# A Fourier mixing layer and a feed-forward layer in one kernel: start-up copies and loads moved, one array laid out anew, batch one's steps renumbered

## The chip, the cores and the metric

The kernel runs on one core of one Trainium2 chip. The metric is the time of one execution in device microseconds (us). Three runs of the kernel before gave 785.98, 788.34 and 785.7 us; their median is 785.98. The core's engines are TensorE (PE in the profile; its weight loads are listed apart as PEld), VectorE (DVE), ScalarE (ACT), GpSimd (POOL) and SyncE (SP). In this kernel GpSimd and SyncE only start transfers (DMAs).

## The reference

For each of 8 batches, x has 3008 rows (the sequence) of 256 channels. The reference computes, in float32,

```
X = rfft(x, axis=1);  Y = X * (filt_r + 1j * filt_i);  y = irfft(Y, n=3008, axis=1)
t = y.reshape(24064, 256)
h = t @ w_in                              # 256 -> 2048
g = max(h, 0) + alpha * min(h, 0)         # alpha: one number for each of the 2048
out = g @ w_out                           # 2048 -> 256
```

The kernel works in 16-bit floats with float32 accumulation and writes float32.

## The kernel before, in words

**The transform.** The length 3008 is split as 94 x 32. Forward stage one is a product over the 94 (table `wf1`, for the first batch `wfx`); it gives 96 rows (48 frequencies, real and imaginary) for each of 32 positions. Then the array is turned so that the 32 positions lie across partitions. Stage two multiplies 64-by-64 blocks (table `twf`, forward), multiplies by the filter on VectorE, and multiplies back (tables `twi` and, for batch zero, `twx`). The result `v` is turned again into `zt`, and a last product over 96 rows (`wi3`) gives `yT`, the transformed tokens with channels across partitions, two batches at a time.

**Two ways to turn.** Batches one to seven (class `Fft`) turn their arrays through memory outside the core: `save_a` writes `a_dram`, `turn_a` reads it back turned; `turn_c` writes `v_dram` and, after the last part, reads `zt`. Batch zero (class `First`) has nothing to hide such trips behind, and turns on TensorE by products with an identity matrix: `turn_at` for the forward side, `half_t` and `piece_t` (through `turn`, line 346) for the inverse one. In both the array to be turned is the stationary operand, so it goes through a weight load.

**Batch zero, in order.** Eight forward pieces (`piece_a`, evicted by ScalarE and VectorE in turn) are made as x arrives. Between them stand warm-up products (`warm`) that compute nothing used. Then come `turn_at`, which moves two or four frequencies' columns from PSUM into `at`; twelve products `piece_b(kp)` (line 299), each followed by one VectorE multiplication by the filter (line 304); twelve products back `piece_c(kp)` (line 324); and `keep_c`, the evictions of their results into `v`. Products of stage two read the table `twd`, which is `twf` with each 32 columns written twice; `twice` makes it in three copies of eight frequencies each. Then `half_t` and `half_d` make a first part of `yT`, and the blocks begin. `piece_t` and `pair_d` of batch zero's other three groups run among the blocks.

**The blocks.** The feed-forward layer runs in 48 blocks of 512 (some 384) tokens, each of 16 steps. A step is one `up` (two products with `w_in`, line 478) and one part of `down` of the block before (products with `w_out`, line 509). Every second step ScalarE evicts two `up` results (line 487) and VectorE makes two products with alpha (line 490); every fourth step VectorE adds four at once (line 492). A batch's transform lies over 96 steps.

**What sets the order.** Nothing is scheduled by a tool: each engine's queue has the order in which the program is written. For the blocks a dictionary `plan` holds, for each step number, the pieces of the transforms to run there; `plan_fft` fills it from lists of steps: forward pieces (`a_at`), the turn (`ta`), loads of the next batch's x (`x_at`), products `piece_b` (`b_at`), `piece_c` (`c_at`, with `turn_c` one step after every second one), and inverse pieces (`d_at`). A piece runs ahead of its step's `up`; forward pieces and `piece_c` run behind the step's `down`, which then comes first.

**Buffers that matter here.** PSUM has eight banks: `hps` two buffers of two banks, `op` two of one, and one buffer `psF` of two. `psF` takes `turn_at`, `piece_t`, `pair_d` and, for batches one on, `piece_b`; there it is held until both VectorE multiplications (lines 186 and 187) have read it. The float32 tile `fst` holds the filter of the first frequencies and lies in the buffer `asb` of the later batches; it is copied into `filt_s` by a DMA on GpSimd's queue (line 428) after the twelve products, and released by that copy. Four copies into `filts_s` (line 431) and two within `filt_s` (line 433) follow on the same queue. `p_x` has four buffers for x.

**Markers.** A tiny `memset` on VectorE into the target of a load makes that load wait for the place that the memset has in VectorE's queue; the load then writes over it.

**Queues at the start.** SyncE's queue has the identity, `wfx`, the first third of `twf`, the eight parts of `fst`, the rest of `twf`, `twi` and `twx`, and small constants. GpSimd's has x of batch zero (eight parts), the filter (24 parts in three groups: frequencies 1 to 3, 4 to 7 and 8 to 11 in the kernel's count), `w_in` (two parts), `w_out` (two parts), x of batch one (eight parts), and the copies named above.

Of the kernel before, what the change touches and what calls it, by code (L numbers as in the profile page):

```python
# [15 lines left out]
NK = 24  # L16
# [34 lines left out]
def kernel(  # L51
# [10 lines left out]
    nc = tc.nc  # L62
# [46 lines left out]
    def load_x(b, c):  # L109
        xs = p_x.tile([N1, 8 * D], FP16, name="xs")  # L110
        for r in (slice(0, 48), slice(48, N1)) :
            nc.gpsimd.dma_start(out=xs[r], in_=xrow(b, c)[r])  # L112
        return xs
# [149 lines left out]
    class First(Fft):  # L263
# [61 lines left out]
                                             u[r, par, i, 128 * f : 128 * f + 128], t[r, 2 * kp + par],  # L325
                                             start=(i == 0), stop=(i == 1))

        def twice(self, ka, kb, copy):
            o = self.twd[:, ka:kb].rearrange("p k (i c m) -> p (k i) c m", i=2, c=2)
            w = twf_s[:, ka:kb].rearrange("p k (i m) -> p (k i) m", i=2)  # L330
            copy(o, w.unsqueeze(2).to_broadcast([128, 2 * (kb - ka), 2, 32]))

        def keep_c(self, kp, evicts, n=2):
            vm = self.vm.rearrange("p (g q k e) -> p g q k e", q=4, k=NK, e=4)
            for e in range(2):
                k = 2 * kp + e
                evicts[e](vm[:, :, :, k : k + 2 * n - 1 : 2],
                          self.ops[e][:, 0:n].rearrange("p k (g q e) -> p g q k e", q=4, e=4))

        def turn(self, pt, i, n):  # L340
            m = self.vm.rearrange("p (g m e) -> p g m e", m=96, e=4)
            for u in range(n):
                for f in range(2):
                    o = 256 * (u % 2) + 128 * f
                    s = n * i + u
                    nc.tensor.matmul(pt[0:96, u // 2, o : o + 128], m[:, 8 * f + s // 4, :, s % 4], id16,  # L346
                                     start=True, stop=True)
# [20 lines left out]
    f0 = First()  # L368
# [1 line left out]
    load_filt(nc.gpsimd, filt_s, 1, 4)  # L370
    load_filt(nc.gpsimd, filt_s, 4, 8)
    load_filt(nc.gpsimd, filt_s, 8, 12)
    for kt in range(2):
        nc.gpsimd.dma_start(out=win_s[:, kt], in_=moe_w_in[kt * 128 : (kt + 1) * 128])
    for q in range(2):
        nc.gpsimd.dma_start(
            out=wout_s[:, 8 * q : 8 * q + 8],
            in_=moe_w_out[1024 * q : 1024 * q + 1024].rearrange("(j p) d -> p j d", p=128))
    for c in range(4):
        xc[(1, c)] = load_x(1, c)  # L380

    def warm(n, pw):
        for _ in range(n):
            nc.tensor.matmul(pw.rearrange("p (r c) -> p r c", r=4), id16,
                             id16.unsqueeze(1).to_broadcast([128, 4, 128]), start=True, stop=True)

    warm(9, bank("o"))
    for i in range(8):
        f0.piece_a(i, both[i % 2], i % 3 < 2)
        if i % 2 == 1:  # L390
            warm((4, 4, 8, 3)[i // 2], bank("o"))
        if i == 1:
            nc.vector.memset(f0.fst[:, 0, :, 0:1], 0.0)
            load_filt(nc.sync, f0.fst, 0, 1)
        if i == 5:
            f0.twice(0, 8, on_act)
            nc.vector.memset(twf_s[:, 8:24, 0:1], 0.0)
            tables(nc.sync, ("twf",), 8, 24)
            tables(nc.sync, ("twi", "twx"), 0, 8)
            tables(nc.sync, ("twi", "twx"), 8, 24)  # L400
            nc.sync.dma_start(out=wi3_s, in_=consts["wi3"].ap())
            nc.sync.dma_start(out=al16, in_=moe_alpha.rearrange("(j p) -> j p", p=128))
            nc.sync.dma_start(out=id32, in_=id32_d.ap())
            nc.sync.dma_start(out=wf1_s, in_=consts["wf1"].ap())
            nc.sync.dma_start(out=sgn_s, in_=sgn_d.ap())
    f0.twice(8, 16, on_act)
    f0.twice(16, 24, on_dve)
    f0.turn_at(0, 1, on_act)
    f0.turn_at(1, 1, on_dve, True)
    warm(2, bank("o"))  # L410
    f0.piece_b(0)
    f0.turn_at(2, 2, on_act)
    f0.piece_b(1)
    warm(2, bank("o"))
    f0.turn_at(4, 2, on_act)
    for kp in range(12):
        if kp < 10:
            f0.piece_b(kp + 2)
        f0.piece_c(kp)
        if kp > 9:  # L420
            f0.keep_c(kp, (on_act, on_act) if kp == 10 else both, 1)
        elif kp % 2 == 1:
            f0.keep_c(kp - 1, (on_act, on_act))
            if kp < 7:
                f0.turn_at(kp + 5, 2, on_act)
        if 7 <= kp < 10:
            warm(2, banks(False)[:, 0])
    nc.gpsimd.dma_start(out=filt_s[:, 0:1], in_=f0.fst)
# [117 lines left out]
            put(d_at[i], f.pair_d, i, on_act)  # L546

    for g, ts, ds, te, de in ((1, (0, 3), (6, 12), on_act, both[::-1]), (2, (19, 23), (25, 28), on_dve, (on_dve, on_dve)),
                              (3, (31, 33), (35, 37), on_act, (on_act, on_act))):
        for i in range(2):  # L550
            put(ts[i], f0.piece_t, 2 * g + i, te)
            put(ds[i], f0.pair_d, 2 * g + i, de[i])
# [7 lines left out]
    def d_steps(p):  # L560
        return [p + t for t in (91, 93, 104, 108, 116, 120, 140, 152)]

    plan_fft(1, range(12, 28, 2), 28, 4, (34, 42, 54, 66), range(38, 74, 6), 0, range(50, 86, 6),
             (91, 93, 97, 100, 111, 121, 142, 154))
    plan_fft(2, (48, 52, 58, 64, 70, 76, 82, 84), 90, 4, (57, 69, 81, 89),
             (106, 116, 126, 136, 148, 158), 7, (116, 126, 136, 148, 158, 172), d_steps(96))
    for b in range(3, NB):
        p = 96 * (b - 1)
# [54 lines left out]
```

## Time and profile before

| what | value |
| --- | --- |
| median of three runs | 785.98 us |
| the profiled execution, and its span | 788.28 us, 786.5 us |
| TensorE busy | 768.0 us (98%) |
| VectorE busy | 595.7 us (76%) |
| ScalarE busy | 585.9 us (74%) |
| first product with `w_in` (line 478) | at 42.59 us |
| TensorE busy from 10 to 20 us | 6.10 us |
| TensorE busy from 60 to 80 us | 19.46 us |
| TensorE busy from 100 to 150 us | 47.85 us |
| granted TensorE clock from 20 to 22 us | 0.50, elsewhere mostly 1.00 |

The profile is of one execution. Times in it count from the start of the span. A busy TensorE means that products are in its pipeline, not that it is at its peak. The chain is the work that ended last, followed back from the end, step by step, to what released it. A line of the timeline or of a wait gives in brackets how long the engine had been idle and what released it; where the release is put down to "issue", the profile shows no cause. The program's names for tiles are used, so `gtb<-twf_s` is a copy from `twf_s` into a part of `gtb`, where `twd` lies.

### The profile page before, as it was taken

What the parts mean: (1) busy time and instruction counts of PE and PEld (TensorE: products, weight loads), DVE (VectorE), ACT (ScalarE), POOL (GpSimd) and SP (SyncE); (2) the same over time, 40 slices, a digit from 0 to 9 for tenths busy, and PEclk for the clock granted to TensorE, in tenths of its full rate; (3) what the DMA queues carried; (4) which work ended last, traced back from release to release, by engine and by line L of the source; (5) the groups of instructions that cost most, each with busy time, mean ns of one, the idle gap of its engine ahead of it and who ended that gap; (6) DMA issues with size and microseconds to landing.
All of it is one profiled execution on the core that took longest, in us unless ns stands there. A gap on an engine that the chain in (4) does not pass through costs nothing.

```text
span 786.5 us, 16089 instructions
## 1 busy us (share of the span) xinstructions
PE 768.0 (98%) x6351; PEld 511.5 (65%) x6351; DVE 595.7 (76%) x1116; ACT 585.9 (74%) x672; POOL 142.8 (18%) x271
## 2 busy tenths in 40 slices
PE   6889998999999999999999999999999999999997
PEld 3556665666666666766666666766666666766665
DVE  2767985788868887788867888688877888766663
ACT  3587787888778887798777887788876777677663
POOL 7420463122202220022201222010100121000000
PEclk9999999999999999999999999999999999999999
DMA  9986599657764657555593655834474233511111
GB/s 179 178 194 161 116 182 223 196 130 163 144 160 109 146 135 148 135 118 130 125 205 84 150 120 132 191 82 108 115 147 129 56 87 92 146 38 28 42 41 54
DMA packets 95083, 100.64 MB, mean 128 GB/s; under 512 B 11280, under 2 KB 82464, under 8 KB 94816
## 3 DMA queue, kind: packets, MB, share of 16 engines
q1 hardware_dynamic: 80368, 70.25, 34.1%
q0 software_dynamic: 14640, 29.38, 21.6%
q8 instruction: 49, 0.80, 0.4%
q14 instruction: 26, 0.21, 0.1%
HBM read 55.28 MB, written 46.66 MB: 130 GB/s over the span
## 4 chain that ended last, share of the span: by engine, by line
PE 93%; DMA 3%; ACT 2%; DVE 1%; issue 1%; SPq 0%; POOL 0%; ACTq 0%; POOLq 0%
PE hps L478 41%; PE op L509 41%; PE hps L155 3%; PE psF L232 3%; PE psF L179 2%; PE hps L210 1%; ACT gtb L487 1%; ACT v L255 1%; PE psF L346 1%; DMA xs<-in_x_dram 1%; DMA fst<-in_filt_r_dram 1%; PE op L324 1%; DMA twf_s<-c_twf 1%; DMA v_dram<-v 1%; DMA zt<-v_dram 0%
## 5 line engine op out<-in xcount | busy, mean ns | idle before, releaser
L487 ACT ACTIVATE gtb<-hps 128x1024 f16<-128x1024 f32 (+1 forms) x384 | 385.7, 1005 | 130.7 <-PE hps L478 129.6
L509 PE MATMUL op<-wout_s,gtb 128*128 128x256 f16 x3008 | 435.7, 273 | 0.1
L478 PE MATMUL hps<-yT,win_s 128*128 128x512 f16 (+1 forms) x1536 | 434.0, 375 | 1.5 <-ACT gtb L487 1.4
L509 PEld LDWEIGHTS <-gtb 128*128 128x128 f16 x3008 | 294.0, 98 | 168.3 <-issue 0.4
L490 DVE TENSOR_SCALAR m<-gtb,alm_s 128x512 f16<-128x512 f16 (+1 forms) x768 | 233.1, 346 | 150.1 <-ACT gtb L487 149.2
L492 DVE TENSOR_TENSOR gtb<-gtb,m 128x2048 f16<-128x2048 f16 (+1 forms) x192 | 231.0, 1203 | 10.4 <-PE hps L478 0.5
L478 PEld LDWEIGHTS <-win_s 128*128 128x128 f16 x1536 | 142.8, 98 | 61.0 <-issue 14.5
L193 POOL DMA_DIRECT2D sw<-ww x144 | 71.1, 501 | 383.1 <-DVE ww L186 380.2
L255 ACT ACTIVATE asb<-hps 96x1024 f16<-96x1024 f32 x56 | 57.1, 1020 | 12.1 <-PE hps L155 11.7
L514 ACT ACTIVATE osb<-op 128x512 f32<-128x512 f32 (+1 forms) x97 | 56.2, 579 | 5.3 <-issue 2.8
L255 ACT ACTIVATE yT<-psF 128x752 f16<-128x752 f32 x59 | 47.0, 797 | 10.8 <-PE psF L232 10.6
L112 POOL DMA_DIRECT2D xs<-in_x_dram x64 | 39.2, 707 | 80.8 <-PE hps L155 69.0
L255 ACT ACTIVATE v<-hps 128x1024 f16<-128x1024 f32 x42 | 43.0, 1024 | 14.2 <-PE hps L210 14.2
L186 DVE TENSOR_TENSOR ww<-psF,filts_s 128x1024 f16<-128x1024 f32 x42 | 51.1, 1218 | 0.0
L187 DVE TENSOR_TENSOR uu<-psF,filt_s 128x1024 f16<-128x1024 f32 x42 | 51.0, 1215 | 0.0
L155 PE MATMUL hps<-xs,wf_s 94*96 94x512 f16 x112 | 33.5, 380 | 0.6 <-ACT asb L255 0.6
L232 PE MATMUL psF<-wi_s,zt 96*128 96x94 f16 x500 | 31.3, 206 | 2.3 <-DMA zt<-v_dram 2.1
L232 PEld LDWEIGHTS <-zt 96*128 96x128 f16 x512 | 28.5, 98 | 5.0 <-DMA zt<-v_dram 2.4
L191 POOL DMA_DIRECT2D uu<-ww x24 | 19.5, 1220 | 38.5 <-DVE uu L187 31.2
L198 DVE TENSOR_TENSOR uu<-uu,sw 128x1024 f16<-128x1024 f16 x36 | 24.7, 685 | 0.0
L179 PE MATMUL psF<-at,twf_s 64*64 64x256 f16 x336 | 17.3, 281 | 0.0
L210 PE MATMUL hps<-uu,twi_s 64*64 64x256 f16 x336 | 16.5, 271 | 0.0
(67 smaller groups left out, 172.1 us busy)
## 6 DMA issues: line engine op xcount, KB each, us to landing
out_dram<-osb SPq DMA_DIRECT2D x160, 128.0 KB
a_dram<-asb SPq DMA_DIRECT2D x28, 384.0 KB
v_dram<-v SPq DMA_DIRECT2D x84, 128.0 KB
zt<-v_dram SPq DMA_DIRECT2D x28, 384.0 KB
sw<-ww POOLq DMA_DIRECT2D x144, 64.0 KB, 2.5
at<-a_dram SPq DMA_DIRECT2D x20, 384.0 KB
xs<-in_x_dram POOLq DMA_DIRECT2D x32, 192.0 KB, 4.6
xs<-in_x_dram POOLq DMA_DIRECT2D x32, 184.0 KB, 5.6
```

The lines of the kernel that those rows point to most:

```text
L155: nc.tensor.matmul(ps[0:96, u], wf1_s, xs[:, o : o + 512], start=True, stop=True)
L186: nc.vector.tensor_mul(ww, px, fs)
L187: nc.vector.tensor_mul(uu, px, f)
L193: nc.gpsimd.dma_start(out=sw[o : o + 32], in_=ww[i : i + 32])
L232: nc.tensor.matmul(ps[:, m], self.zt[:, 8 * g + 4 * mh + m, dh * 128 : dh * 128 + 128], wi3_s, start=True, stop=True)
L255: nc.scalar.activation(o, i, AF.Copy)
L478: nc.tensor.matmul(self.hps[:, j % 2, 0:tn], win_s[:, kt, j * 128 : (j + 1) * 128], yT[:, kt, self.t0 : self.t0 + tn], start=(kt == 0), st ...
L487: nc.scalar.activation(g[:, 2 * i : 2 * i + 2], self.hps[:, :, 0:tn], AF.Copy)
L490: nc.vector.tensor_scalar(m[:, 2 * i + h], g[:, 2 * i + h], 0.0, a, OP.min, OP.mult)
L492: nc.vector.tensor_add(g, g, m)
L509: nc.tensor.matmul(self.op[:, si - s0], self.gts[k][:, 128 * si : 128 * si + 128], wout_s[:, k], start=(si == s0 and k == 0), stop=(si == ...
L514: nc.scalar.activation(osb[:, 0:m], self.op[:, 0:m], AF.Copy)
```

## The change

It has five parts.

1. The second and third copy of `twice` move from before `turn_at` to behind the second and third `turn_at` pair that feeds `piece_b`, and the third goes from VectorE to ScalarE. The first stays at its place on ScalarE, written after the loads of the tables. These loads, with their marker, are written two pieces earlier, and two of eight warm-up products go.
2. The loads of `w_in`, `w_out` and of batch one's x stand inside the loop over the twelve products, behind a marker in `w_in`'s tile that VectorE writes after the eighth `piece_b` (kp = 7) has been multiplied.
3. The array `vm` that `keep_c` writes and `turn` reads has its innermost index `e` moved outermost: the 96 columns of one weight load now lie side by side (before, every fourth element), and one eviction's elements that lay four in a row now lie 1536 elements apart.
4. The last group of batch zero is turned at steps 32 and 34 (before 31 and 33), its inverse pieces run at 39 and 45 (before 35 and 37). Batch one's `piece_b` and `piece_c` run two steps sooner (36, 42, ... and 48, 54, ...).
5. Batch two's forward pieces run at 50, 56, 62, 68, 74, 80, 82, 84 (before 48, 52, 58, 64, 70, 76, 82, 84).

```
-        def twice(self, ka, kb, copy):
+        def twice(self, ka, kb):
...
-            copy(o, w.unsqueeze(2).to_broadcast([128, 2 * (kb - ka), 2, 32]))
+            on_act(o, w.unsqueeze(2).to_broadcast([128, 2 * (kb - ka), 2, 32]))
...
         def keep_c(self, kp, evicts, n=2):
-            vm = self.vm.rearrange("p (g q k e) -> p g q k e", q=4, k=NK, e=4)
+            vm = self.vm.rearrange("p (e g q k) -> p g q k e", q=4, k=NK, e=4)
...
         def turn(self, pt, i, n):
-            m = self.vm.rearrange("p (g m e) -> p g m e", m=96, e=4)
+            m = self.vm.rearrange("p (e g m) -> p g m e", m=96, e=4)
...
-    for kt in range(2):
-        nc.gpsimd.dma_start(out=win_s[:, kt], in_=moe_w_in[kt * 128 : (kt + 1) * 128])
-    for q in range(2):
-        nc.gpsimd.dma_start(
-            out=wout_s[:, 8 * q : 8 * q + 8],
-            in_=moe_w_out[1024 * q : 1024 * q + 1024].rearrange("(j p) d -> p j d", p=128))
-    for c in range(4):
-        xc[(1, c)] = load_x(1, c)
...
         if i % 2 == 1:
-            warm((4, 4, 8, 3)[i // 2], bank("o"))
+            warm((4, 4, 6, 3)[i // 2], bank("o"))
...
-        if i == 5:
-            f0.twice(0, 8, on_act)
+        if i == 3:
             nc.vector.memset(twf_s[:, 8:24, 0:1], 0.0)
             tables(nc.sync, ("twf",), 8, 24)
...
-    f0.twice(8, 16, on_act)
-    f0.twice(16, 24, on_dve)
+        if i == 5:
+            f0.twice(0, 8)
     f0.turn_at(0, 1, on_act)
     f0.turn_at(1, 1, on_dve, True)
     warm(2, bank("o"))
     f0.piece_b(0)
     f0.turn_at(2, 2, on_act)
+    f0.twice(8, 16)
     f0.piece_b(1)
     warm(2, bank("o"))
     f0.turn_at(4, 2, on_act)
+    f0.twice(16, 24)
     for kp in range(12):
...
+        if kp == 5:
+            nc.vector.memset(win_s[:, 0, 0:2], 0.0)
+            for kt in range(2):
+                nc.gpsimd.dma_start(out=win_s[:, kt], in_=moe_w_in[kt * 128 : (kt + 1) * 128])
+            for q in range(2):
+                nc.gpsimd.dma_start(
+                    out=wout_s[:, 8 * q : 8 * q + 8],
+                    in_=moe_w_out[1024 * q : 1024 * q + 1024].rearrange("(j p) d -> p j d", p=128))
+            for c in range(4):
+                xc[(1, c)] = load_x(1, c)
...
-                              (3, (31, 33), (35, 37), on_act, (on_act, on_act))):
+                              (3, (32, 34), (39, 45), on_act, (on_act, on_act))):
...
-    plan_fft(1, range(12, 28, 2), 28, 4, (34, 42, 54, 66), range(38, 74, 6), 0, range(50, 86, 6),
+    plan_fft(1, range(12, 28, 2), 28, 4, (34, 42, 54, 66), range(36, 72, 6), 0, range(48, 84, 6),
              (91, 93, 97, 100, 111, 121, 142, 154))
-    plan_fft(2, (48, 52, 58, 64, 70, 76, 82, 84), 90, 4, (57, 69, 81, 89),
+    plan_fft(2, (50, 56, 62, 68, 74, 80, 82, 84), 90, 4, (57, 69, 81, 89),
```

## The prediction, made before the changed kernel ran

> **What bounds the kernel now.** I read the page first: its chain, the work that ended last, is TensorE's for 93% of the span, and its slices show TensorE nearly full everywhere but in the first five and at the end. So the change can win time in two places: the first 60 us, where TensorE waits, and single waits of TensorE later. The timeline, the windows, the waits and the groups by line say what ends those waits.
>
> The chain by engine, then the timeline of the start (start, duration, engine, line, what; in brackets the idle time before and its releaser; "issue" is a piece of the chain in order of time):
> ```profile
> PE 93%; DMA 3%; ACT 2%; DVE 1%; issue 1%; SPq 0%; POOL 0%; ACTq 0%; POOLq 0%
> ...
> 13.32 0.34 SPq L365 DMA_DIRECT2D twf_s<-c_twf  x1
> 17.59 1.06 ACT L255 ACTIVATE gtb<-twf_s 128x1024 f16<-128x1024 f16 x1 [3.20 <-DMA twf_s<-c_twf]
> 19.18 0.41 PE L299 MATMUL hps<-at,gtb 64*64 64x256 f16 x8 [3.12 <-ACT at L255]
> 23.40 1.54 POOL L122 DMA_DIRECT2D filt_s<-in_filt_i_dram  x3 [0.23 <-DMA filt_s<-in_filt_i_dram]
> 24.94 1.12 POOL L374 DMA_DIRECT2D win_s<-in_moe_w_in_dram  x2
> 31.01 1.03 issue
> 47.47 1.98 POOL L431 DMA_DIRECT2D filts_s<-filt_s  x4 [6.27 <-DMA filt_s<-fst]
> 51.54 1.02 ACT L255 ACTIVATE asb<-hps 96x1024 f16<-96x1024 f32 x1
> ```
> The second table lands at 17.50; ScalarE copies it before it takes the first turned piece out of PSUM, so the first product of stage two starts at 19.18, after 3.12 us of idle TensorE. At 31.01 there is a gap without a named cause. The copy out of fst has landed at 47.47; the first asb eviction, into the buffer that fst held, follows at 51.54.
>
> Weight loads by line (ns min/median/max), then the later timeline:
> ```profile
> L346 PEld LDWEIGHTS <-v x64: 163/186/188, 38.4 to 76.2; 128*96 128x96 f16 x64
> L155 PEld LDWEIGHTS <-wf_s x112: 119/123/126, 50.3 to 556.6; 94*96 94x96 f16 x112
> ...
> 58.32 0.84 PE L346 MATMUL psF<-id,v 128*96 128x128 f16 x8
> 73.22 0.84 PE L346 MATMUL psF<-id,v 128*96 128x128 f16 x8 [0.54 <-DVE yT L258]
> 87.17 0.41 PE L179 MATMUL psF<-at,twf_s 64*64 64x256 f16 x8
> 90.89 1.22 DVE L187 TENSOR_TENSOR uu<-psF,filt_s 128x1024 f16<-128x1024 f32 x1
> 136.87 0.51 PE L232 MATMUL psF<-wi_s,zt 96*128 96x94 f16 x8 [2.13 <-DMA zt<-v_dram]
> ```
> A load of 96 columns that lie 8 bytes apart takes 186 ns, a dense one 123. The one psF buffer, written at 87.17, is free when the second product ends at 92.11. At 136.87 TensorE has waited 2.13 us for batch one's last turn: its only large wait after 60 us.
>
> **The change, part by part.** The sum is made against the profiled execution: 788.28 us, span 786.5 and 1.8 around it. The median of the three runs is 785.98, 2.3 lower.
>
> *Tables.* The second load and its marker stand two pieces earlier. On SP's queue a load goes out when the one eight places before it has landed: the table left at 13.32, when the first fst part (issued 8.60, 4.64 us to landing) was in, and the load issued at 17.52 followed the table's landing at 17.50. So the table still leaves at 13.3, with all that follows it on SP: nothing won there. But it is no longer awaited: the first turned piece can go when VectorE's last eviction ends (13.91 + 0.96 = 14.87), 0.4 earlier because two warm products of 0.21 before it are gone (the last x piece was in at 12.5). Turn 0.4 and eviction 0.58 later the first product starts near 15.7, 3.5 sooner. The three copies now all cost ScalarE 1.05; it then waits for products anyway, so I charge nothing, and 2.1 if that cover is gone.
>
> *Filters take half of it back.* Product four needs the second filter group. POOL's queue keeps the same rule of eight: with its last issue at 24.4 the group is surely in, the part before it at 23.35. Product four thus starts near 24.0; before it was 23.35 + 2 x 1.15 = 25.65. Gain 1.65. Then VectorE runs products of 1.15 each. The gap of 1.03 at 31.01 falls among the weight transfers, which now start later; I take it as gone (ends 0 and 1.03). Sixteen turns before 40 us save 0.4 (below). In all 3.1 sooner at 42 us.
>
> *Weights and x loads.* They wait for a marker on VectorE (0.07 us) behind product seven: 24.0 + 4 x 1.15 = 28.6, so the first leaves near 28.7, not 24.94: 3.8 later. Landing took 8.1 at most for the second win part: 37.4, needed at 42.59 - 3.1 = 39.5. The last wout: 43, needed near 52. The first x pieces (11.9 to landing): 46, needed near 48. All fit. Behind them on POOL stands the copy out of fst: before, 22.5 us from first weight load to its landing, with the DMA share near 1 from 26 to 46. Part of that were the last filter loads (24 to 28 moved 100 and 133 GB/s, later windows 200), so I take 21.5: landing 50.2 (ends 49.3 and 51.2). The first asb eviction waits for that landing, and everything behind it on ScalarE, TensorE's evictions too. So of 3.1 only 51.54 - 50.2 = 1.3 is left (ends 0.3 and, should nothing wait, 3.1).
>
> *Dense turned array.* Eight turns take 0.84, so (0.84 - 0.25) / 7 = 84 ns apart; eight turns of dense 128 columns (line 290) 0.62, 57 ns apart. A dense 96-column load (123 ns) is nearer to the 98 of those than to 186, so I take 57: 0.21 for eight. Four such groups lie in the part where TensorE is full: 0.85 (ends 0 and 0.85; all dense loads are shorter, so no loss). [...]
> ScalarE's ten evictions into this array (0.54 each) now write single elements far apart. Runs of four elements cost no more than dense ones (0.81 for 768), single ones no row shows; I take nothing. Rival four has the price.
>
> *Third group, steps 31 to 37.* A turn at 32 no longer meets VectorE's late eviction: 0.54 saved. Batch one's first product at 36 runs near 78; its input, issued from 72.6 at some 200 GB/s, has its first quarter in near 76.5. But now the group's two inverse pieces come three steps behind products in the same psF: at 39 behind 36, at 45 behind 42. Three steps are 2.96 us (81.51 to 84.47). Products of batch one held psF 3.79, 4.94, 3.48, 4.43, 3.27 and 4.44, longer each time that VectorE's add of line 492 came just before, as before step 36. So TensorE, in order, waits 1.5 to 2.0 at one and 0.3 to 0.9 at the other: I take 2.4 lost (ends 0.6 and 3.5).
>
> *Batch one sooner.* Between its last product and its first inverse piece lie 13 steps instead of 11 and three forward pieces instead of two: 2 x 0.87 + 0.43 = 2.2 more cover for the 2.13 wait. The last ScalarE eviction also no longer queues behind an output one, nor the stores behind it on SP. The wait goes: 2.1 (ends 1.7 and 2.2).
>
> Sum: -1.3 - 0.85 - 0.54 + 2.4 - 2.1 = -2.4, so 785.9 for such an execution and 785.98 - 2.4 = 783.6 for the median.
>
> **Rivals.**
> 1. The DMA chain doesn't bind: the fst copy lands before it is asked for. For it: DMA idles ahead of the late start; against: DMA was full to 46. Then 3.1 instead of 1.3: 781.8.
> 2. No psF waits: VectorE has caught up at 36 and 42. For it: no inverse pieces load ScalarE at 35 and 37; against: the shortest hold seen, 3.27, exceeds 2.96. Then 2.4 less: 781.2.
> 3. The dense array doesn't do what it should: turns stay 84 ns apart. 784.4.
> 4. The other side: scattered writes slow ScalarE's evictions of v. At three times 0.54, two evictions and a turned piece take 4.27 for each two products of VectorE's 2.3: 2.0 late in each of three rounds, 0.9 in each of two, some 2 in the tail, 9.9 in all; instead of 1.3 won, 6.8 are lost: 791.7. It decides from about twice the time, 1.1 us. For it: no row has such writes; against: runs of four are free. [...]
>
> **How the numbers follow.** Likeliest, with 45%: 783.6, its own range 781.9 to 785.5. Rival one 17%, two 17%, three 12%, four 9%. The good ends together give -6.1 and 779.9, the bad ones +1.5 and 787.5; only rival four lies outside. A measurement of this kernel tells about 0.5% from no change (its runs spread 0.34%): 782.05 and 789.9. Faster: most of rivals one and two and a fifth of the likeliest, 32%. Slower: most of rival four, 8%. The rest 60%.
>
> **What would show it.** The first L299 product near 15.7; product four of L304 near 24; win_s issued near 28.7; filts_s released by the fst copy near 50, and the first asb eviction waiting for that DMA; L346 loads near 123 ns; L232 at steps 39 and 45 waiting for DVE L187; no wait for zt near 135; v evictions still 0.54. It is wrong if weights or x land after their first use, if TensorE's clock (0.50 at 20 to 22 us) falls in the new waits, or if ScalarE's evictions of v lengthen.

## The result, and the profile after

The changed kernel takes 811.12 us (median of six executions, 807.18 to 816.12); the kernel before took 787.19 us beside it (785.7 to 793.32). The ratio is 1.0286, with a 95% interval from 1.0229 to 1.0343: slower, far outside the predicted range. The profiled execution took 808.31 us, its span is 806.5 (before: 786.5).

Nearly the whole difference lies ahead of the feed-forward layer. The first product with `w_in` (now line 481) starts at 61.9 us instead of 42.6, 19.3 later; from there to the end the kernel takes 744.6 us instead of 743.9.

The changed kernel's chain of work by engine; ScalarE has 6% of it where it had 2%:
```profile
PE 88%; ACT 6%; DMA 2%; DVE 2%; issue 1%; POOL 0%; ACTq 0%; DVEq 0%; POOLq 0%
```
The same kernel's timeline (start, duration, engine, line, what; in brackets the idle time before and what ended it), at the start and around steps 39 and 45:
```profile
15.59 0.41 PE L299 MATMUL hps<-at,gtb 64*64 64x256 f16 x8
...
20.42 4.61 ACT L255 ACTIVATE v<-op 128x512 f16<-128x512 f32 x2
...
23.75 1.22 DVE L304 TENSOR_TENSOR uu<-hps,filt_s 128x1024 f16<-128x1024 f32 x1 [2.47 <-DMA filt_s<-in_filt_r_dram]
...
26.80 4.62 ACT L255 ACTIVATE v<-op 128x512 f16<-128x512 f32 x2 [0.93 <-PE op L324]
...
101.54 0.51 PE L232 MATMUL psF<-wi_s,zt 96*128 96x94 f16 x8 [1.80 <-DVE uu L187]
...
108.56 0.51 PE L232 MATMUL psF<-wi_s,zt 96*128 96x94 f16 x8 [0.84 <-DVE uu L187]
```
The first product of stage two starts at 15.59, as planned. Then two evictions of `v` take 4.61 us; before, one took 0.54. From 20.42 on they come every 6.4 us (20.42, 26.80, 33.20, 39.62), and TensorE waits for them. Its waits for these evictions in the first 60 us (sum, number, longest), in the changed kernel and then in the kernel before:
```profile
PE op L324 <- ACT v L255: 16.0, 10, 2.0
```
```profile
PE op L324 <- ACT v L255: 0.3, 1, 0.3
```

Groups by line, each shape apart, of the changed kernel (busy, mean ns of one, idle time before):
```profile
L255 ACT ACTIVATE v<-op 128x512 f16<-128x512 f32 x10 | 23.1, 2554 | 5.5 <-PE op L324 5.5
...
L258 DVE CAST v<-psF 128x256 f16<-128x256 f32 x1 | 1.3, 1302 | 8.2 <-ACT v L255 8.2
```
The same two groups of the kernel before:
```profile
L255 ACT ACTIVATE v<-op 128x512 f16<-128x512 f32 x10 | 5.4, 594 | 4.0 <-PE op L324 4.0
...
L258 DVE CAST v<-psF 128x256 f16<-128x256 f32 x1 | 0.4, 424 | 2.0 <-ACT v L255 2.0
```
So the ten took 5.4 us before and take 23.1 now, and the one 424 ns before and 1302 now. (The mean counts the overlap of successive instructions; below, the cost of one eviction is busy time by count, so 2.31 us after and 0.54 before.) VectorE, with the same writes, is slowed as ScalarE is.

Busy time of PE, PEld, DVE, ACT and POOL by stretches of the changed kernel, then the granted clock, the DMA share and GB/s:
```profile
20.00:30.00 10.00, 4.90 (x92) 3.24 (x90) 4.89 (x4) 9.07 (x6) 3.04 (x6) 0.63 0.61 90
30.00:60.00 30.00, 17.40 (x212) 9.25 (x212) 8.80 (x9) 21.82 (x15) 9.57 (x17) 0.50 0.82 143
```
ScalarE is the full engine from 20 to 30 us. TensorE, waiting each round, is granted half its clock from 24 to 60 us, so its own part of a round takes longer as well: eight products of line 299 last 0.64 us where they last 0.41 at the full clock.

### The profile page after: what moved, and what is told of

Its sections match the earlier page's. It is cut to its first block, busy times and chain, and to the rows that moved or that the text cites. A ratio compares the mean times of both kernels' runs of the same rounds, so it can differ in the third digit from the quotient of the medians.

```text
span 806.5 us, 16086 instructions
## 1 busy us (share of the span) xinstructions
PE 773.3 (96%) x6349; PEld 512.2 (64%) x6349; DVE 596.8 (74%) x1116; ACT 606.3 (75%) x673; POOL 142.2 (18%) x271
## 4 chain that ended last, share of the span: by engine, by line
PE 88%; ACT 6%; DMA 2%; DVE 2%; issue 1%; POOL 0%; ACTq 0%; DVEq 0%; POOLq 0%
PE hps L481 39%; PE op L512 39%; ACT v L255 3%; PE hps L155 3%; PE psF L232 3%; PE psF L179 2%; ACT gtb L490 1%; PE hps L210 1%; DMA uu<-ww 1%; DMA xs<-in_x_dram 1%; PE op L324 1%; DMA zt<-v_dram 1%; DVE ww L186 1%; DVE uu L187 1%; DVE m L493 1%
## 5 line engine op out<-in xcount | busy, mean ns | idle before, releaser
L112 POOL DMA_DIRECT2D xs<-in_x_dram x64 | 39.2, 709 | 91.1 <-PE hps L155 79.4
L186 DVE TENSOR_TENSOR ww<-psF,filts_s 128x1024 f16<-128x1024 f32 x42 | 51.1, 1217 | 0.0
L232 PEld LDWEIGHTS <-zt 96*128 96x128 f16 x512 | 28.7, 99 | 6.8 <-DVE uu L187 3.2
L255 ACT ACTIVATE v<-op 128x512 f16<-128x512 f32 (+1 forms) x12 | 25.5, 2376 | 6.2 <-PE op L324 6.2
L191 POOL DMA_DIRECT2D uu<-ww x24 | 19.3, 1229 | 40.8 <-DVE uu L187 35.6
L304 DVE TENSOR_TENSOR uu<-hps,filt_s 128x1024 f16<-128x1024 f32 x11 | 13.4, 1222 | 17.0 <-PE hps L299 14.6
```

Of the source, the lines that this page charges most:

```text
L186: nc.vector.tensor_mul(ww, px, fs)
L232: nc.tensor.matmul(ps[:, m], self.zt[:, 8 * g + 4 * mh + m, dh * 128 : dh * 128 + 128], wi3_s, start=True, stop=True)
L255: nc.scalar.activation(o, i, AF.Copy)
```

## The experiments

The theory after the result (S in the expectations): the scattered two-byte writes into the turned array slow its evictions, and that is the loss. The rivals put the loss elsewhere: into loads that come too late, or into TensorE's clock. Each kernel ran beside the kernel before on the same chip, and ratios are against that. On these chips the kernel before has medians of 790.65 to 792.52, where the chip of the prediction had 785.98; the section on the clock shows what that goes with. Line numbers move by a few between kernels.

**1. The old layout in the changed kernel.**
```
-            vm = self.vm.rearrange("p (e g q k) -> p g q k e", q=4, k=NK, e=4)
+            vm = self.vm.rearrange("p (g q k e) -> p g q k e", q=4, k=NK, e=4)
...
-            m = self.vm.rearrange("p (e g m) -> p g m e", m=96, e=4)
+            m = self.vm.rearrange("p (g m e) -> p g m e", m=96, e=4)
```


> The changed kernel with the old layout of the turned array; all else of the change stays. Theory S (the single-element writes are the whole loss): evictions of v back at 0.54 us from 2.31, turns back at 84 ns apart, and the rest of the change as first forecast without its dense loads: 783.6 + 0.85 = 784.5 us, between 782 and 788. Rival L (the late weight and x loads, with the copy out of fst behind them, cost as well): first feed-forward product no sooner than 45 us, time above 790. Rival C (the two warm products and the moved table copies let TensorE's clock fall, which slows the start by itself): clock near 0.5 from 20 to 40 us with the old layout too, time above 790.

Measured: 793.9 against 790.86, ratio 1.0034 [1.0008, 1.0059]. The ten evictions are back at 5.4 us, the first `w_in` product at 41.4. So the layout is nearly all of the loss (1.0286 / 1.0034 = 1.025), but what is left is no gain: the other four parts cost 0.3%. Of the expectations, S's evictions came and its time, at most 788, did not. L's sign, a first product no sooner than 45 us, did not come, and C's only in part: the clock is 0.50 from 26 to 32 us and 1.00 from 34 to 40. The timeline of this kernel shows two of the places:
```profile
51.26 1.02 ACT L255 ACTIVATE asb<-hps 96x1024 f16<-96x1024 f32 x1 [0.77 <-PE hps L481]
51.39 1.95 POOL L434 DMA_DIRECT2D filts_s<-filt_s  x4 [6.91 <-DMA filt_s<-fst]
52.33 0.59 PE L155 MATMUL hps<-xs,wf_s 94*96 94x512 f16 x2 [1.45 <-ACT asb L255]
...
140.82 0.51 PE L232 MATMUL psF<-wi_s,zt 96*128 96x94 f16 x8 [2.98 <-DMA zt<-v_dram]
```
The copy out of `fst`, issued at 43.9 and 7.2 us on its way, landed at 51.1 and held the first `asb` eviction, and TensorE behind it. And the wait for `zt`, which was to go, is 2.98 instead of 2.13.

**2. The new layout alone, in the kernel before** (the diff of experiment 1 the other way round).

> The kernel before with the dense layout alone. Theory S: evictions of v at 2.31 us instead of 0.54, ten of 512 and four of 256 elements, 24 us of busy time more on ScalarE and VectorE, of which VectorE's products and the old waits hide some 3: 805 to 812 us. Rivals L and C: the layout alone costs less than 8 us, 795 or below.

Measured: 813.67 against 790.86, ratio 1.0272 [1.0236, 1.0309]. By form:
```profile
L255 ACT ACTIVATE v<-op 128x512 f16<-128x512 f32 x10 | 23.1, 2558 | 6.6 <-PE op L324 6.6
```
The same evictions, the same loss, without any of the other parts; the time is a little above the 805 to 812 expected of S. As the cause of the main loss L and C are out, for they had 795 or below.

**3. The eviction's order turned, so that two frequencies that lie 4 bytes apart in memory are written one after the other.** The product's columns are written two frequencies at a time, k and k + 2, whose elements lie 4 bytes apart in the new layout.
```
-            vm = self.vm.rearrange("p (e g q k) -> p g q k e", q=4, k=NK, e=4)
+            vm = self.vm.rearrange("p (e w k) -> p e w k", k=NK, e=4)
...
-                          self.ops[e][:, 0:n].rearrange("p k (g q e) -> p g q k e", q=4, e=4))
+                          self.ops[e][:, 0:n].rearrange("p k (g q e) -> p e (g q) k", q=4, e=4))
```


> The changed kernel, same dense layout, but each eviction of v goes through its elements in another order: the two frequencies innermost, 4 bytes apart and mostly in one 16-byte piece, so that two writes follow each other there. PSUM is then read with steps of 1 KB. [...] If every two-byte write that does not adjoin the one before pays by itself: evictions stay at 2.3 us, time 805 to 812. [...]

Measured: 802.59, ratio 1.0133 [1.0106, 1.016]; the ten evictions take 12.6 us, 1.26 each. Same number of elements, same places, another order: from 23.1 us the time nearly halves. So the order of the writes counts, not the array's size or place. The 2.3 us of the expectation, and with them 805 to 812, did not come. The kernel is still 11.7 us above the kernel before: the first `w_in` product is at 50.7, and the clock is at half for 20.5 us from 23.5 on and for 6.8 us more from 47 on.

**4. The price of a write by its distance.** Copies of 512 elements from one PSUM buffer, four of each, added behind the last block of the kernel before; nothing else runs then. These copies write over data that is no longer needed, and the kernel's own time says nothing (872.24 us).

> The kernel before with copies of 512 elements from PSUM added behind its end, four of each pattern, so its time is not to be compared; only the mean time of each pattern is read. Theory S: dense 0.58 us, runs of four 0.58, the changed kernel's order 2.3 on ScalarE and about 2.5 on VectorE, single elements 16 or 32 bytes apart also 2.3, single elements 4 bytes apart near 0.6 if the 16-byte line decides and 2.3 if each lone two-byte write pays. Rival R (the order in which PSUM is read is the cause): the dense write with the scattered read is slow too, single elements with a dense read are quick. Four-byte single elements: 0.6 if only two-byte writes pay, 2.3 if the line decides.

The groups of these copies (busy, mean ns), ScalarE's (ACT) and VectorE's (DVE):
```profile
L613 ACT ACTIVATE yT<-op 128x512 f16<-128x512 f32 x4 | 9.5, 2384 | 0.1
L627 DVE CAST yT<-op 128x512 f16<-128x512 f32 x4 | 9.5, 2372 | 0.1
...
L609 ACT ACTIVATE yT<-op 128x512 f16<-128x512 f32 x4 | 5.2, 1302 | 0.1
L632 ACT ACTIVATE fprobe<-op 128x512 f32<-128x512 f32 x4 | 4.3, 1066 | 0.1
...
L603 ACT ACTIVATE yT<-op 128x512 f16<-128x512 f32 x4 | 2.5, 628 | 0.1
...
L599 ACT ACTIVATE yT<-op 128x512 f16<-128x512 f32 x4 | 2.4, 596 | 0.1
```

| line | what is written | ScalarE, ns | VectorE, ns (its line) |
| --- | --- | --- | --- |
| 599 | two-byte elements, dense | 596 | 692 (619) |
| 601 | runs of four, every 64 bytes | 597 | 691 (621) |
| 603 | runs of two, every 32 bytes | 628 | 691 (623) |
| 605 | single, every 32 bytes | 2304 | 2292 (625) |
| 607 | single, every 16 bytes | 2431 | |
| 609 | single, every 8 bytes | 1302 | |
| 611 | single, every 4 bytes | 737 | |
| 613 | the changed kernel's order | 2384 | 2372 (627) |
| 615 | the order of experiment 3 | 1344 | |
| 617 | dense, but read from PSUM in scattered order | 597 | |
| 632 | four-byte elements, single, every 16 bytes | 1066 | |

The changed kernel's order costs what lone elements cost, some 4.5 ns each (2304 / 512), on both engines alike; reading in scattered order costs nothing (597 ns against 596). The more single elements share 16 bytes, the less one costs: 4.7 ns for one there (2431 / 512), 2.5 for two (1302 / 512), 1.4 for four (737 / 512). But an adjoining pair, one to every 32 bytes, costs 2.5 ns for both (628 / 256), less than one lone element, and so does a lone four-byte element (1066 / 512 = 2.1). So neither rule of the expectation, a price for each change of 16 bytes or one for each lone two-byte write whatever its distance, fits all rows; what the price is paid for stays open.

**5. The start alone, with the old layout and the old steps:** tables and weight loads as in the changed kernel, everything else as before.
```
-                              (3, (32, 34), (39, 45), on_act, (on_act, on_act))):
+                              (3, (31, 33), (35, 37), on_act, (on_act, on_act))):
...
-    plan_fft(1, range(12, 28, 2), 28, 4, (34, 42, 54, 66), range(36, 72, 6), 0, range(48, 84, 6),
+    plan_fft(1, range(12, 28, 2), 28, 4, (34, 42, 54, 66), range(38, 74, 6), 0, range(50, 86, 6),
...
-    plan_fft(2, (50, 56, 62, 68, 74, 80, 82, 84), 90, 4, (57, 69, 81, 89),
+    plan_fft(2, (48, 52, 58, 64, 70, 76, 82, 84), 90, 4, (57, 69, 81, 89),
```
(against experiment 1's kernel)

> The kernel before with the moved table copies and the late weight and x loads; old layout, old steps. Theory P (the late loads hand the won time back): first feed-forward product near 41.4 us instead of 42.6, but the first asb eviction held near 51.3 by the copy out of fst, TensorE's clock falling to 0.5 behind it; time 0 to 1 us above the kernel before. Rival Q (the loss left with the old layout all comes from the steps): the start alone is 1 us or more faster than before.

Measured: 792.21 against 791.5, ratio 1.0005 [0.9982, 1.0029]. The first `w_in` product is at 39.2, 3.4 sooner than in the profile of before. The timeline shows where it is handed back:
```profile
50.17 1.02 ACT L255 ACTIVATE asb<-hps 96x1024 f16<-96x1024 f32 x1 [1.95 <-DVE m L493]
50.30 1.95 POOL L434 DMA_DIRECT2D filts_s<-filt_s  x4 [6.13 <-DMA filt_s<-fst]
51.24 0.59 PE L155 MATMUL hps<-xs,wf_s 94*96 94x512 f16 x2 [2.64 <-ACT asb L255]
...
137.56 0.81 PE L232 MATMUL psF<-wi_s,zt 96*128 96x94 f16 x8 [2.94 <-DMA zt<-v_dram]
```
The first eviction is named as released by VectorE, which had long been done; it starts when the copy out of `fst` lands (issued at 43.6, landed 6.4 us later), as GpSimd's next line shows. TensorE stands 2.64 us behind it.

**6. The tables alone:** weights loaded early as before, old layout, old steps.

> The kernel before with the moved table copies alone; weights load as before. Theory P: first feed-forward product near 41.5 us, the copy out of fst landed near 47.5, first asb eviction near 50.4 without a wait; time 1 us or a little more below the kernel before. Rival T (the moved copies themselves cost, since TensorE then waits for filters and its clock falls): no gain, within 0.4 us of before or above.

Measured: 789.55, ratio 0.9975 [0.9949, 1.0001], a gain of the expected size that is not quite clear of none. The copy out of `fst` lands at 47.6 and TensorE waits 0.57 at `asb` instead of 2.64. The first `w_in` product is at 40.8 here, and the `zt` wait has grown to 4.04.

**7. The steps alone:** the start and the layout as before, third group, batch one and batch two as in the changed kernel.

> The kernel before with the new steps alone. Theory P: TensorE waits 2.6 us for psF at steps 39 and 45 and saves 0.5 at 31; the wait for zt stays at 2 to 3 us because batch two's later pieces release x loads in front of it; time 2 to 3 us above the kernel before. Rival Z (the longer wait for zt seen with the old layout was chance): the wait for zt goes, time within 0.8 us of before.

Measured: 792.9, ratio 1.0023 [0.9998, 1.0048]. The waits at steps 39 and 45 are there (1.80 and 0.85), and two more, from the timeline:
```profile
125.04 0.41 PE L210 MATMUL hps<-uu,twi_s 64*64 64x256 f16 x6 [1.65 <-DMA uu<-ww]
139.37 0.81 PE L232 MATMUL psF<-wi_s,zt 96*128 96x94 f16 x8 [2.55 <-DMA zt<-v_dram]
```
The last product back, at step 78, comes before its DMA-swapped half is there; and the `zt` wait, 2.13 before, is not gone. The time is 1.4 above the kernel before beside it, where 2 to 3 were expected.

**8. The tables, and steps set apart from each other:** on experiment 6's kernel, batch one's products keep clear of the third group's inverse pieces at 35 and 37, and batch two's forward pieces do not move later.
```
-    plan_fft(1, range(12, 28, 2), 28, 4, (34, 42, 54, 66), range(38, 74, 6), 0, range(50, 86, 6),
+    plan_fft(1, range(12, 28, 2), 28, 4, (34, 42, 54, 66), (38, 43, 48, 54, 60, 66), 0, range(48, 84, 6),
...
-    plan_fft(2, (48, 52, 58, 64, 70, 76, 82, 84), 90, 4, (57, 69, 81, 89),
+    plan_fft(2, (46, 50, 56, 62, 68, 74, 82, 84), 90, 4, (57, 69, 81, 89),
```


> A mended version: moved table copies; weights as before; old layout; the last group of batch zero at its old steps 31 to 37; batch one's products at 38, 43, 48, 54, 60, 66 and back at 48 to 78; batch two's forward pieces at 46, 50, 56, 62, 68, 74, 82, 84, so that they keep their distance to batch one's last turn. Theory P: no wait for psF above 0.6 us, the wait for zt below 0.5, time 3 us below the kernel before (2 to 4). Rival Z: the wait for zt stays near 2 us and only the tables' 1 us is won.

Measured: 785.14 against 791.5, ratio 0.9918 [0.9889, 0.9946]. From 60 to 150 us two waits of TensorE are left: 0.5 at step 31 and 1.6 for `zt`. The `zt` wait was expected below 0.5, and the gain is 6.4 where 2 to 4 were expected; the section on the clock divides it. One of the seven executions took 1601.71 us, at a full clock; the ratio leaves it out, and nothing on record shows its cause.

**9. Two x loads held back,** on experiment 8's kernel: a marker makes batch three's third and fourth x load wait for VectorE at steps 93 and 95.
```
+        if b == 3 and c > 1:
+            nc.vector.memset(xs[:, 0:2], 0.0)
...
-    plan_fft(2, (46, 50, 56, 62, 68, 74, 82, 84), 90, 4, (57, 69, 81, 89),
+    plan_fft(2, (46, 50, 56, 62, 68, 74, 82, 84), 90, 4, (57, 69, 93, 95),
```


> The mended version (steps apart) with batch three's third and fourth x load held by markers on VectorE until steps 93 and 95, that is until batch one's last turn has been read back. Theory X (x loads in front of the turn's write and read make the wait for zt, which then depends on DMA traffic and not on steps): the wait for zt falls from 1.6 us to below 0.5, the last eviction of v to the first zt product takes below 12 us. Rival S2 (stores or the turn's own length make it): the wait stays between 1 and 3 us. The time differs from the mended version's by less than 2 us either way.

Measured: 784.43 against 792.52, ratio 0.9896 [0.987, 0.9921]. The timeline of experiment 8's kernel, then of this one:
```profile
126.28 1.04 POOL L112 DMA_DIRECT2D xs<-in_x_dram  x2 [8.64 <-PE hps L155]
127.45 1.72 SPq L227 DMA_DIRECT2D zt<-v_dram  x4
...
132.68 0.51 PE L232 MATMUL psF<-wi_s,zt 96*128 96x94 f16 x8 [1.61 <-DMA zt<-v_dram]
```
```profile
127.89 1.72 SPq L229 DMA_DIRECT2D zt<-v_dram  x4
...
133.45 0.50 PE L234 MATMUL psF<-wi_s,zt 96*128 96x94 f16 x8
...
137.44 2.14 POOL L114 DMA_DIRECT2D xs<-in_x_dram  x4 [19.50 <-DVE xs L112]
```
The x loads went just ahead of the reading of `zt`. Held back, they leave TensorE with no `zt` wait. Experiment 12, which also holds them, has none either; experiments 10 and 11, which do not, have 1.23 and 0.61, so the wait varies between executions. From the last product back to the first product on `zt` pass 11.1 us in both profiles with the loads held and 12.2 to 12.9 in the three without. So in these kernels the `zt` wait is made by x loads, which batch two's forward pieces release.

**10. Five products that compute nothing,** on experiment 8's kernel, where TensorE waits for the second filter group.
```
+        if kp == 2:
+            warm(5, banks(False)[:, 0])
```


> The mended version with five warm-up products (some 1.1 us) behind the third product back, where TensorE otherwise idles for the second filter group. Theory K (the clock falls to 0.5 near 26 us in some executions because of that idle time, as in the runs with the old layout and with the tables alone, and costs 1 to 2 us then): clock 1.00 through 20 to 34 us, first feed-forward product near 39 us, median 0 to 1 us below the mended version's. Rival: the warm products delay product six: first feed-forward product 1 us later.

Measured: 784.2, ratio 0.9898 [0.9871, 0.9926]. The granted clock is 1.000 in the mean of each of the six executions. The first `w_in` product starts at 39.9, 1.0 later than in experiment 8's profile. So both came, the clock of theory K and the delay of its rival.

**11. The quick load without the slow write,** on experiment 8's kernel: `e` is split in two bits, and one stays innermost. Each eviction writes adjoining pairs; a load's columns lie 4 bytes apart instead of 8.
```
-            vm = self.vm.rearrange("p (g q k e) -> p g q k e", q=4, k=NK, e=4)
+            vm = self.vm.rearrange("p (a w k b) -> p w k a b", k=NK, a=2, b=2)
...
-                evicts[e](vm[:, :, :, k : k + 2 * n - 1 : 2],
-                          self.ops[e][:, 0:n].rearrange("p k (g q e) -> p g q k e", q=4, e=4))
+                for i in range(n):
+                    evicts[e](vm[:, :, k + 2 * i], self.ops[e][:, i].rearrange("p (w a b) -> p w a b", a=2, b=2))
...
-            m = self.vm.rearrange("p (g m e) -> p g m e", m=96, e=4)
+            m = self.vm.rearrange("p (a g m b) -> p g a b m", m=96, a=2, b=2)
```


> The mended version with a third layout of the turned array: elements in pairs of two, so that a weight load's columns lie 4 bytes apart and each eviction writes adjoining pairs; an eviction of two frequencies becomes two of one. By the copies timed alone (runs of two cost 0.63 us for 512 elements against 0.60): evictions of 256 elements near 0.4 us each, so ScalarE has some 2.5 us more in all, mostly beside VectorE's products. If a weight load's time follows the distance of its columns: 140 to 160 ns instead of 186, turns 60 to 75 ns apart instead of 84, 0.3 to 0.8 us won where TensorE is full. If only side-by-side columns are quick: 186 ns and 84 as before, and the time up to 1 us above the mended version's.

Measured: 783.3, ratio 0.989 [0.9863, 0.9918]. By form:
```profile
L255 ACT ACTIVATE v<-op 128x256 f16<-128x256 f32 x22 | 6.9, 406 | 6.7 <-PE op L324 6.7
...
L346 PEld LDWEIGHTS <-v 128*96 128x96 f16 x64 | 4.4, 124 | 2.2 <-issue 1.0 <-DVE v L258 0.5
```
Loads take 124 ns as with the dense array, and an eviction of 256 takes 406, where the old layout has 382: what the layout was to bring to the loads, and more than either case of the expectation gave them, is to be had with pairs.

**12. Experiments 8 to 11 together.**

> Tables moved, weights early, third group and batch two's pieces at their old steps, batch one's products at 38 and 43 to 66 and products back at 48 to 78, the marker that holds batch three's third and fourth x load, the five filling products after the third product back, and the array of turned pieces in adjoining pairs, all together. If the three additions gain in different places they add: apart from them this kernel came out at 0.9918, and they took off 0.0022 (the zt wait), 0.0020 (the clock held at the start) and 0.0028 (quick weight loads), so 0.985, some 779.5 us where the kernel before takes 791.5, with no zt wait, loads of line 348 near 123 ns, the clock at 1.00 from 20 to 40 us and the first w_in product near 40. If the additions only repeat one gain, above all if the shorter time for two of them was the scatter of executions, it stays at 0.989 (782.8 us). At 0.992 or more none of the three gains stands.

Measured: 782.87 us (781.97 to 784.11) against 790.65, ratio 0.9903 [0.9873, 0.9934]. No `zt` wait, loads of 123 ns. But the three gains did not add up to 0.985: the ratio is no better than that of experiment 11. In its profile TensorE waits 1.06 at 19.49 for `twi` and 0.54 at 20.23 for `twx`, the clock falls at 21, and the first `w_in` product is at 40.8. It has the lowest median of all kernels here; whether it is better than experiment 11's these runs cannot tell.

### The clock, and the times at equal clock

The granted clock is read here in stretches of 2 us. Where it falls in these profiles, it falls to 0.50, and a fall lasts 3.4 us or a whole number of times that: twice, 6.8 us (experiments 9 and 11), or eleven times, 37.5 (the changed kernel, from 22.7 to 60.2). The one fall of the kernel before, by windows (clock third from the end):
```profile
18.00:20.00 2.00, 0.82 (x13) 0.62 (x13) 0.98 (x3) 1.13 (x2) 1.01 (x2) 0.88 1.00 241
20.00:22.00 2.00, 2.00 (x18) 0.87 (x15) 1.68 (x2) 1.03 (x1) 0.00 (x0) 0.50 1.25 228
22.00:24.00 2.00, 2.00 (x47) 1.36 (x47) 1.06 (x2) 1.01 (x1) 1.61 (x4) 0.77 0.79 110
```
(0.12 + 0.50 + 0.23) x 2 / 0.50 = 3.4. And the fall behind experiment 1's `zt` wait:
```profile
140.00:142.00 2.00, 1.18 (x14) 0.95 (x15) 0.00 (x0) 0.63 (x1) 0.00 (x0) 0.92 1.05 260
142.00:144.00 2.00, 2.00 (x13) 1.35 (x12) 1.00 (x3) 0.87 (x2) 0.00 (x0) 0.50 1.03 350
144.00:146.00 2.00, 2.00 (x17) 1.42 (x16) 0.51 (x1) 1.49 (x2) 0.00 (x0) 0.72 0.93 358
```
(0.08 + 0.50 + 0.28) x 4 = 3.4 again. `zt` waits of 2.08, 2.55, 2.94, 2.98, 3.04 and 4.04 (experiments 2, 7, 5, 1, 3, 6) are each followed by such a fall; those of 2.66 (experiment 4), 2.13 (before), 1.61 and 1.23 (experiments 8 and 10) and two shorter ones are not. So no length of the wait decides it; what does, no run here shows. Experiment 2's wait, with the clock at 0.50 from 162 to 164 us, and experiment 4's, with 1.00 from 130 to 144:
```profile
160.41 0.51 PE L232 MATMUL psF<-wi_s,zt 96*128 96x94 f16 x8 [2.08 <-DMA zt<-v_dram]
```
```profile
136.09 0.51 PE L232 MATMUL psF<-wi_s,zt 96*128 96x94 f16 x8 [2.66 <-DMA zt<-v_dram]
```
The stalls at `asb` in experiments 1 and 5 (1.45 and 2.64) are followed by one from 52 to 56 us, and the idle time at the start by one in most profiles, in some of them by one of 6.8 us (experiments 1, 2, 9 and 11). By an estimate from these figures a fall where TensorE is the bound costs half of 3.4, 1.7 us, on top of the wait.

On the later chips the kernel before is slower, and over its executions there its time goes with the mean granted clock, from 786.0 at 1.000 to 796.4 at 0.988. One common slope, fitted to the 141 executions of the kernel before and of the full kernels without the slow writes, is 695 us for the whole clock, or 0.7 us for each 0.001 of it (so 1.5 us for one fall, 0.0022 of the span), and the scatter about it is 1.2 us. The fit takes the chips as alike at equal clock; the kernel before alone comes out at 786.5 to 787.6 on them, so differences under one microsecond are not shown. With it the kernels can be compared at full clock (standard errors 0.3 for before, 0.4 to 0.5 for the others); the falls that a change itself brings or saves are then left out:

| kernel | mean clock | median, us | at full clock, us | against before |
| --- | --- | --- | --- | --- |
| before | 0.9940 | 791.5 | 787.1 | |
| 1 all but the layout | 0.9936 | 793.9 | 789.2 | +2.1 |
| 5 tables, late weights | 0.9932 | 792.2 | 787.2 | +0.1 |
| 6 tables | 0.9952 | 789.6 | 786.0 | -1.2 |
| 7 steps | 0.9948 | 792.9 | 789.1 | +1.9 |
| 8 tables, steps apart | 0.9987 | 785.1 | 783.8 | -3.4 |
| 9 and x held back | 0.9972 | 784.4 | 782.1 | -5.0 |
| 10 and filling products | 1.0000 | 784.2 | 784.4 | -2.8 |
| 11 and pairs | 0.9970 | 783.3 | 781.6 | -5.6 |
| 12 all of these | 0.9988 | 782.9 | 782.1 | -5.1 |

Within these errors the parts add: start +0.1 and steps +1.9 make experiment 1's +2.1. Holding back x is worth 783.8 - 782.1 = 1.7 (error 0.7), near the `zt` wait of 1.61. The filling products cost 0.6 at equal clock, about their error, and keep a clock that falls in some executions without them. Experiments 8 to 12 win twice: shorter waits, and fewer falls behind them.

## Why the prediction was wrong, point by point

**Dense array: the step that failed.** "ScalarE's ten evictions into this array [...] single ones no row shows; I take nothing." The evictions took 2.31 us each instead of 0.54. Rival four named the mechanism and its deciding point, 1.1 us; it was given 9% and priced at three times 0.54, where it was 4.3 times. With 2.31 its own working gives 2 x 2.31 + 1.03 = 5.65 for a round instead of VectorE's 2.3, so 3.35 late in three rounds, 2.3 in two, some 3.3 in the tail: 18.0. Less the 3.1 won, 14.9; measured were 19.3 at the first `w_in` product. The rest was not in the rival: a round took 6.4, for ScalarE also waited 0.93 in each for TensorE's products back, which ran at half clock. How much of the 0.93 the clock makes no run separates. The choice between the ends, "runs of four are free", was the wrong neighbour: a run of four writes to adjoining places, a single element adjoins nothing. The trace of before could not decide it, so its place was the range, not a chance of 9%.

That lone writes slow an eviction was the author's supposition in rival four, without a row for it. Experiment 4 shows it, and where it ends: 512 lone elements 32 bytes apart cost 2304 ns and two to each 16 bytes still 1302, against 596 for dense ones, while adjoining pairs, one to each 32 bytes, cost 628.

**Dense array: the loads.** Right: 123 ns, and eight turns in 0.61, so (0.61 - 0.22) / 7 = 56 ns apart where 57 was predicted. The same load takes 186 ns with its columns 8 bytes apart (before) and 124 at 4 (experiment 11).

**Tables, Filters.** Right up to product four: first product at 15.59 (15.7), product four at 23.75 (24.0), released by the filter's DMA. Without the slow writes the first `w_in` product came at 41.6 to 38.9, so 1.0 to 3.7 sooner than in the profile of before, where 3.1 was predicted. The spread goes with the clock: it falls near 25, behind the wait for the filter, in the profiles with 40.8 to 41.6 (experiments 1, 6, 9 and 11) and not in those with 38.9 and 39.2 (8 and 5). VectorE's wait for the filter is also longer in the four, 2.58 to 3.48 against 1.55 and 1.78. The prediction names the clock as a danger and does not price it.

The 3.1 was also counted from a single execution, and a late one. The unchanged start is on record three times, in the profiles of before and of experiments 7 and 4:
```profile
42.59 1.46 PE L478 MATMUL hps<-yT,win_s 128*128 128x512 f16 x6
```
```profile
40.44 1.46 PE L478 MATMUL hps<-yT,win_s 128*128 128x512 f16 x6
```
```profile
41.28 1.46 PE L478 MATMUL hps<-yT,win_s 128*128 128x512 f16 x6
```
The gap of 1.03 at 31.01, which the prediction took as gone because the weights move, is absent from the other two, where they do not move. Against the mean of the three, 41.4, the eight profiles of experiments 1, 5, 6 and 8 to 12 (mean 40.5) win 0.9, not 3.1, and that within their scatter.

**Weights.** The chain was right: in experiment 1 `win_s` left at 28.75 (28.7), the copy out of `fst` landed at 51.1 (50.2, at worst 51.2) and the `asb` eviction waited for it. In experiment 5 that eviction starts at 50.17, 1.37 sooner than in the profile of before, so "1.3 is left" held up to there, counted from that late execution; in experiments 7 and 4, with the old start, it is at 49.39 and 50.23. For the whole kernel it did not hold: experiment 5 is at +0.1. From the first `w_in` product on, experiment 5's profile takes 750.3 us instead of 743.9. Of these 6.4 two falls of the clock, at 52 and at 138, are 3.4, the longer `zt` wait 0.8, and some 2.2 are left for the stall at `asb`, where the prediction had 1.8. So the stall was sized nearly right, and what it does to the clock was not in the sum. Experiment 6 against 5 gives 1.2 us (error 0.5) for loading the weights early.

**Third group.** Right: 1.80 + 0.84 = 2.64 waited at steps 39 and 45 where 2.4 was predicted, and experiment 7 has 1.80 and 0.85. Experiment 8 has neither.

**Batch one sooner: the second step that failed.** "The wait goes: 2.1". Counting cover in steps assumed that the transfer takes a fixed time. It took longer instead: from the last product back to the first product on `zt` the five profiles with the old steps (before and experiments 2, 4, 5, 6) have 11.75 to 13.65 us, with waits of 2.08 to 4.04, and experiments 1, 3 and 7 have 14.76, 14.82 and 14.33. Experiment 9 shows what can fill the time. Batch two's pieces, moved to 80 to 84, released x loads that ran just ahead of the reading (129.0 and 133.1, with `zt` issued at 134.5, in experiment 1). A wait that nobody had foreseen came too: step 78, for `uu<-ww`, 1.65 in experiment 7 and 0.75 in the changed kernel. In the changed kernel, with the same steps and loads, the way was 12.29 and the `zt` wait only 0.52; why it was shorter there stays open. At equal clock the steps lose 1.9 (experiment 7), and the third group's 2.64 - 0.54 = 2.1 accounts for that: batch one's products brought nothing on balance.

The other four parts at equal clock, then: the start was to win 1.3 and stands at +0.1 (experiment 5), the steps were to win 0.54 - 2.4 + 2.1 = 0.24 and stand at +1.9 (experiment 7). Even without the dense array the change would not have been faster, and the likeliest case would have failed by these two. The bad end of the sum, +1.5, comes out only if the 0.54 is not won either; with it, the bad ends named add up to +0.96.

## What to carry to other kernels

Before an array is laid out for its reader, price the writer: two-byte elements should leave an engine in adjoining pairs at least (628 ns for 512 on ScalarE, where lone ones took 2304), and a layout that keeps one bit innermost may serve both sides (in experiment 11 a load of 124 ns instead of 186, an eviction of 406 instead of 382). A step moved earlier only gains if what it waits for is not itself held by traffic that the same change releases (from the last product back to the first product on `zt` the new steps took 14.3 to 14.8 us in experiments 1, 3 and 7, though 12.29 in the changed kernel, and the old ones 11.75 to 13.65); look at what else is on the DMA queues in that window. Waits of TensorE of 1.45 to 4.04 us had a fall of the clock to 0.50 behind them here, by the fit some 1.5 us more for each, and others of up to 2.66 had none; these runs do not say beforehand which one will. And a gap without a cause in one profile may be that execution's alone: a second profile of the unchanged kernel tells.

## What the hardware showed that was not expected

- In experiment 4 a lone two-byte write, 32 bytes from the next, costs some 4.5 ns on ScalarE and VectorE alike (2304 and 2292 ns for 512); on ScalarE a lone four-byte one, 16 bytes from the next, costs some 2 ns (1066 for 512) and an adjoining pair of two-byte ones, 32 bytes from the next pair, 2.5 ns for both (628 for 256 pairs).
- A weight load of 96 columns takes 123 ns with dense columns (the changed kernel), 124 and 123 with columns 4 bytes apart (experiments 11 and 12), 186 at 8 bytes (before).
- The granted clock falls to 0.50 for 3.4 us or a whole number of times that (3.4, 6.8 and 37.5 us), and the spread of the executions of the kernel before on the later chips, 786 to 796 us, goes mostly with its mean (1.000 to 0.988), with a scatter of 1.2 us about the fit.
